# Loading and transposing the first attention group in other pieces, in a kernel of attention and four experts

## The chip, the cores and the metric

The kernel runs on one core of a Trainium2 chip. The metric is the device time of one execution, in microseconds. Beside the timed runs one execution was profiled; its trace gives each instruction's start and duration on the engines: PE (matrix multiplication), PEld (loading of PE's stationary operand), DVE (vector), ACT (activation functions), POOL (general purpose) and SP (here only issuing transfers). PSUM is the memory into which PE writes; SBUF is the working memory.

## The reference

Two steps. The first is attention for 4 batches and 8 heads over 768 positions with 64 elements per head. Heads 0, 2 and 6 ("retrieval") attend causally to everything; the others ("streaming") to the first 4 positions and a window of 64.

```python
scores = scale * np.matmul(q, k.transpose(0, 1, 3, 2))
stream_keep = causal & (is_sink | in_win)
a = np.exp(scores - max); a = a / (sum(a) + 1e-9)
attn_out = np.matmul(a, v)
```

The second feeds the 3072 resulting rows of 512 elements through 4 experts and adds them with normalised weights p:

```python
h = np.maximum(x @ w1[e], 0.0)          # 512 -> 1024
out += p[:, e:e + 1] * (h @ w2[e])      # 1024 -> 512
```

## The kernel before, in words

Attention is done in eight groups: a batch b and one half c of its 768 positions (384 queries). Group 0 is batch 0, first half. The experts ("MoE") work on the transposed attention output xT of a group, in four chunks of 128 features (ct 0 to 3); head h lands in chunk h % 4, half h // 4. PE runs one order, written out at build time: first group 0's attention alone, then the experts' matmuls with the later groups' attention steps put between them by a planner that adds up estimated durations. All engines run in the order in which the instructions are recorded; a semaphore holds an instruction, and all behind it on its engine, until its inputs and its buffer are ready.

**Loads.** Group 0's q and k are loaded as float32 through the queues of SP and ACT, one transfer per head, each a row of 64 elements (256 bytes) per partition and tile (`rows_of`, lines 411 and 424). The tiles q32 and k32 lie in hA, which later holds expert activations. Values and weights go through POOL's queue, which converts to float16 on the way: `load_v` (lines 304 and 310), `load_w1` (line 335, two halves per expert) and `load_w2` (lines 357 and 362). POOL issues them in the order of the text: v of head 0, then the masks bC and bS (lines 457 to 509), v of heads 2, 1, 3, 4, 6, 5, 7, then w1(0) and w2(0), some memsets, w1(1). `landed` makes POOL wait for a transfer before it asks for more. A queue has eight completion semaphores in turn, so a transfer is issued only when the one eight before it has landed.

**Group 0's attention.** `transposes(hp)` (lines 576 to 626) takes the pair of heads 2hp and 2hp+1: three transpositions of 128x128 float32 for q and three for k on PE, into a bank of PSUM, then copies to float16: q to qT, the keys of a retrieval head to kR, those of a streaming head to kS (with the first four positions repeated as "sinks", line 626). `scores(h)` (line 693) multiplies keys and queries, adds the mask as another matmul (line 705) and takes the exponential on ACT (line 711, es). `values` multiplies by v: for retrieval heads with a column of ones that gives the sum (line 756), then `rs`, its reciprocal and a product on DVE (lines 781 to 785), and `x_transposes` (line 805) turns the result back into xT. For streaming heads the product (line 828) comes with the sum in the other half of the partitions; ACT takes Ln and Exp(-) of it (lines 846 and 856) and DVE multiplies (line 851). Heads 3 and 4 share one Exp over 128 partitions (line 861). `sink_row` (line 318) copies four rows of v. `warm_up` (line 448) issues matmuls on zeros where PE would wait.

PSUM banks come from three pools: pA (4, scores and transposes), pV (2, values) and pO (2, warm-up, values of the second half, x_transposes and later expert output).

**Order in group 0 before:** transposes(0), scores(0), transposes(1), scores(2), scores(1) with values(0), transposes(2), scores(3) with values(2), x_transposes(0), scores(4), transposes(3), values(1), scores(5) with values(3), scores(6) with values(4), scores(7) with values(6), values(5), x_transposes(6) and values(7). Then expert 0's first layer starts (line 1095), its second layer is line 1116. Group 1's q and k are loaded as float16 in runs of three consecutive positions and transposed by matmuls with the identity (line 579).

Of the kernel before, what the change touches and what calls it, by code (L numbers as in the profile page):

```python
# [11 lines left out]
FP32 = mybir.dt.float32  # L12
# [7 lines left out]
def kernel(  # L20
# [33 lines left out]
    nc = tc.nc  # L54
# [260 lines left out]
    def sink_row(h):  # L315

        t = v_tiles(0, 0, h)
        nc.vector.tensor_copy(
            out=t[0:NS, :, own_v(h)],
            in_=v_s32[:, h : h + 1, :].to_broadcast([NS, TC, D]),  # L320
        )
# [10 lines left out]
    def load_w1(e, f0, f1):  # L332
        x = moe_w1[e].rearrange("(u c d) f -> u d c f", u=2, c=DMP)
        for u in range(2):
# [65 lines left out]
    def rows32(n):  # L400
        x = hA[:, n * 6 * H * D : (n + 1) * 6 * H * D].bitcast(FP32)
        return x.rearrange("p (j h d) -> p j h d", j=3, h=H)
# [3 lines left out]
    for h in range(H):  # L406
        if h == 2:
            nc.sync.dma_start(
                out=v_s32, in_=v[0, :, 0:NS, :].rearrange("h r d -> r h d")
            )  # L410
        nc.sync.dma_start(out=k32[:, :, h, :], in_=rows_of(k, 0, h, 0))
        if h == HP:

            nc.scalar.add_instruction(
                mybir.InstLoadActFuncSet(
                    name=nc.get_next_instruction_name(),
                    engine=ENG.Activation,
                    act_func_set_id=[x.name for x in SETS].index(
                        "natural_log_exp_and_others"
                    ),  # L420
                )
            )
        eng = nc.scalar if h < HP else nc.sync
        eng.dma_start(out=q32[:, :, h, :], in_=rows_of(q, 0, h, 0))
# [8 lines left out]
    nc.vector.memset(warm.bitcast(FP32), 0.0)  # L433
    nc.vector.memset(eps, 1e-9)
# [5 lines left out]
    zero(nc.vector, kS[:, 0, :, :, :])  # L440
# [14 lines left out]
    def mask_c(x, keep, drop):  # L455

        gp.memset(x, keep)
# [7 lines left out]
    def mask_s(x, n, keep, drop):  # L465

        gp.memset(x, keep)
        gp.affine_select(
            out=x, in_=x, compare_op=ALU.is_ge, fill=drop,
            base=R0, pattern=[[0, n], [1, TQ]], channel_multiplier=-1,  # L470
        )
        gp.affine_select(
            out=x, in_=x, compare_op=ALU.is_ge, fill=drop,
            base=NW - 1 - R0, pattern=[[0, n], [-1, TQ]], channel_multiplier=1,
        )
        gp.memset(x[0:R0, :, :], drop)
        gp.memset(x[0:NS, :, 0:TK], keep)
# [28 lines left out]

    mask_c(bC, 0.0, -60000.0)
    mask_s(bS[:, 0:2, :], 2, 0.0, -60000.0)
    gp.tensor_copy(out=bS[:, 2, :], in_=bS[:, 1, :])
    load_v(0, 0, [2, 1, 3, 4, 6, 5, 7])  # L510
    load_w1(0, 0, F)
# [46 lines left out]
    def attention(b, c):  # L558
# [8 lines left out]
        def transposed(x, hp):  # L567

            if first or hp > 1:
                ps = bank()  # L570
            else:
                ps = pV.tile([P, 512], FP32, name="pV", bufs=2)
            for j in range(3):
                o = ps[:, j * P : (j + 1) * P]
                if first:
                    nc.tensor.transpose(o, x[:, j, 2 * hp : 2 * hp + 2, :], ident32)
                    continue
                for u in range(2):
                    nc.tensor.matmul(
                        out=o[u * D : (u + 1) * D, :],  # L580
                        lhsT=x[:, 2 * hp + u, j, :],
                        rhs=ident16,
                        start=True,
                        stop=True,
                    )
            return ps

        def transposes(hp):
            both_at_once = [] if first else [transposed(x, hp) for x in (qt16, k16)]
            for x, is_k in ((q32 if first else qt16, 0), (k32 if first else k16, 1)):  # L590
                ps = transposed(x, hp) if first else both_at_once[is_k]
                if not is_k:
                    op = nc.scalar.copy if first and hp < 2 else nc.vector.tensor_copy
                    op(out=rows_in_order(qTs[b, c][:, hp, :]), in_=cols(ps))
                    if first:
                        yield t_ns
                    continue
                for u in range(2):
                    h = 2 * hp + u
                    r = slice(u * D, (u + 1) * D)  # L600
                    if RETR[h]:
                        nc.vector.tensor_copy(  # L602
                            out=rows_in_order(
                                kR[i][r, c, RH.index(h), :, :].rearrange(
                                    "r t x -> r (t x)"
                                )
                            ),
                            in_=cols(ps[r, :]),
                        )
# [3 lines left out]
                    if first:  # L613
                        x_in = x_in.rearrange("r (t x) -> r t x", x=TK)
                    else:
                        x_in = x_in.rearrange("r (j t p) -> r j t p", j=3, t=TC)
                        x_out = x_out.rearrange("r t (p j) -> r j t p", j=3)
# [8 lines left out]
                    op(out=sinks, in_=src.to_broadcast([D, TC, NS]))  # L626
                yield 2 * t_ns if first else 3 * t_ns

        def rows_in_order(x):

            return x if first else x.rearrange("r (p j) -> r j p", j=3)

        def cols(x):
            x = x[:, 0:CH]
            return x if first else x.rearrange("r (j p) -> r j p", j=3)

# [42 lines left out]

        es_of = {}  # L680
# [130 lines left out]
        def values(h):  # L811
# [30 lines left out]
            pair = first and h in (3, 4)  # L842
            if not pair or u == 0:
                rc_of[0] = att.tile([P, CH], FP32, name="rc", bufs=2)
            rc = rc_of[0]
# [12 lines left out]
            elif u == 0:  # L858
                scale_of[0] = scale
            else:  # L860
                nc.scalar.activation(out=rc, in_=rc, func=AF.Exp, scale=-1.0)
                later(scale_of[0], g)
# [805 lines left out]
```

## Time and profile before

| | |
|---|---|
| median of 3 runs | 376.27 us (376.0 to 377.43) |
| profiled execution | 377.82 us, span 376.1 us |
| PE busy | 367.1 us (98%) |
| DVE, ACT, POOL busy | 281.6, 227.3, 112.9 us |
| first expert matmul (line 1095) | 21.50 us |
| last wait of PE for weights | about 54.6 us |
| software queue (POOL), hardware queue of SP | 85824 and 36276 packets |

Times in the trace are in microseconds from the start of the span. In a timeline the columns are start, time from the first start to the last end of the merged instructions, engine, line, operation, output<-input, shapes and types, number, and in brackets the idle time of the engine before it and what ended it. In a view of waits a line is: who waited for whom, total, number of waits, longest. In a chain a piece is start, duration and what ran. A group's view of one line gives the shortest, median and longest duration in nanoseconds and the first and last start. PE's ends are modelled: matmuls overlap, so spacing between starts is the better price of one.

### The profile page before, as it was taken

How to read it: one execution, taken by the hardware profiler on the slowest of the kernel's cores; microseconds unless marked ns; L12 is line 12 of the kernel's file. 1: busy time of each engine (PE TensorE's matmuls, PEld its weight loads, DVE VectorE, ACT ScalarE, POOL GpSimd, SP SyncE). 2: the span in 40 equal slices, each digit the busy share in tenths (PEclk: the TensorE clock that was granted, in tenths of full speed). 3: DMA queues.
4: the chain of work that ended last, by engine and by line, in shares of the span. 5: the costliest groups of instructions: out<-in, count | busy, mean ns of one | idle time of the engine just before them, and what ended most of it. 6: DMA issues, size and time to landing. Idle time of an engine off the chain costs nothing.

```text
span 376.1 us, 10310 instructions
## 1 busy us (share of the span) xinstructions
PE 367.1 (98%) x4221; PEld 312.4 (83%) x4221; DVE 281.6 (75%) x589; ACT 227.3 (60%) x475; POOL 112.9 (30%) x155
## 2 busy tenths in 40 slices
PE   8889999999999999999999999999999999999996
PEld 4755556568998999999989899988899998998996
DVE  7774768697788569868657858957767968989882
ACT  3863478557785785765676955774678362450630
POOL 8923664793058038115601650320000000000000
DMA  8999999999599579988904991971220200300101
GB/s 157 159 208 207 179 186 194 180 201 121 90 104 164 97 83 133 153 111 63 205 12 61 169 156 16 131 129 12 68 72 2 92 24 2 114 2 0 58 3 58
DMA packets 123748, 39.25 MB, mean 104 GB/s; under 512 B 113728, under 2 KB 116356, under 8 KB 123700
## 3 DMA queue, kind: packets, MB, share of 16 engines
q0 software_dynamic: 85824, 19.01, 58.6%
q1 hardware_dynamic: 36276, 19.18, 23.3%
q8 instruction: 33, 0.54, 0.7%
q10 hardware_dynamic: 1600, 0.39, 0.5%
q14 instruction: 15, 0.12, 0.1%
HBM read 44.89 MB, written 6.34 MB: 136 GB/s over the span
## 4 chain that ended last, share of the span: by engine, by line
PE 78%; DMA 12%; DVE 5%; POOL 3%; issue 1%; ACT 0%; DVEq 0%; POOLq 0%
PE pO L1409 29%; PE pA L1229 20%; PE pO L1258 9%; PE pO L1116 5%; DMA q<-in_q_dram 5%; PE pA L693 4%; DMA w2sb<-in_moe_w_dram 4%; PE pA L1095 3%; DMA w1sb<-in_moe_w_dram 2%; PE pV L1258 2%; PE pA L1258 2%; DVE xs L1180 2%; PE pV L828 2%; PE pV L756 2%; DMA xT<-x_pair 1%
## 5 line engine op out<-in xcount | busy, mean ns | idle before, releaser
L1409 PEld LDWEIGHTS <-hA 128*128 128x128 f16 x1104 | 104.9, 98 | 11.9
L1229 PE MATMUL pA<-xs,w1sb 128*128 128x256 f16 x768 | 97.1, 272 | 0.0
L1229 PEld LDWEIGHTS <-w1sb 128*128 128x128 f16 x768 | 71.7, 98 | 7.3
L1409 PE MATMUL pO<-w2sb,hA 128*128 128x256 f16 x640 | 76.8, 272 | 0.0
L711 ACT ACTIVATE es<-pA 128x384 f16<-128x384 f32 (+2 forms) x122 | 59.2, 512 | 26.4 <-PE pA L693 23.2
L1238 ACT ACTIVATE hA<-pA 128x512 f16<-128x512 f32 x96 | 57.2, 597 | 29.6 <-PE pA L1229 27.3
L306 POOL DMA_DIRECT2D vS<-in_v_dram x30 | 29.6, 986 | 113.7 <-PE pV L828 110.5
L1409 PE MATMUL pO<-tsb,hA 128*128 128x256 f16 x464 | 56.8, 272 | 0.0
L1180 DVE TENSOR_TENSOR xs<-xT,pB 128x1024 f16<-128x1024 f16 (+1 forms) x49 | 47.0, 977 | 3.7 <-DMA xT<-x_pair 3.7
L1014 DVE TENSOR_TENSOR hA<-hA 128x1024 f16<-128x1024 f16 x60 | 39.4, 684 | 0.6 <-PE pO L1409 0.3
L1108 ACT ACTIVATE hA<-pA 128x384 f16<-128x384 f32 (+1 forms) x64 | 22.2, 385 | 20.3 <-PE pA L1095 20.2
L1258 PEld LDWEIGHTS <-w1sb 128*128 128x128 f16 x512 | 31.3, 98 | 2.1 <-DVE xs L1014 0.8
L1095 PE MATMUL pA<-xT,w1sb 128*128 128x384 f16 (+1 forms) x256 | 30.4, 272 | 2.0 <-DMA w1sb<-in_moe_w_dram 1.9
L1116 PE MATMUL pO<-w2sb,hA 128*128 128x512 f16 x128 | 30.6, 379 | 0.1
L1095 PEld LDWEIGHTS <-w1sb 128*128 128x128 f16 x256 | 19.5, 98 | 11.0 <-issue 2.6
L1429 ACT COPY s<-pO 128x256 f32<-128x256 f32 x31 | 11.5, 372 | 27.3 <-PE pO L1409 21.8
L851 DVE TENSOR_TENSOR xT<-pV,rc 64x384 f16<-64x384 f32 x37 | 20.5, 554 | 9.3 <-ACT rc L856 6.8
L722 DVE TENSOR_TENSOR es<-es,mS 128x384 f16<-128x384 f16 (+1 forms) x40 | 13.8, 344 | 18.0 <-ACT es L711 17.9
L846 ACT ACTIVATE rc<-pV,eps 64x384 f32<-64x384 f32 x37 | 21.3, 575 | 7.0 <-PE pV L828 6.4
L1275 DVE CUSTOM_DVE_ANT_0 hA<-pO,s 128x512 f16<-128x512 f32 x26 | 17.7, 688 | 9.9 <-PE pO L1258 8.5
L1268 ACT COPY s<-pO 128x512 f32<-128x512 f32 x39 | 22.7, 588 | 3.2 <-PE pO L1258 3.0
L693 PE MATMUL pA<-qT,kR 128*128 128x128 f16 (+2 forms) x141 | 23.1, 261 | 0.4 <-DVE kR L602 0.4
(170 smaller groups left out, 527.6 us busy)
## 6 DMA issues: line engine op xcount, KB each, us to landing
pB<-p_rows SPq DMA_DIRECT2D x10, 512.0 KB
out_dram<-o SPq DMA_DIRECT2D x19, 256.0 KB
w1sb<-in_moe_w_dram POOLq DMA_DIRECT2D x8, 512.0 KB, 9.2
w2sb<-in_moe_w_dram POOLq DMA_DIRECT2D x4, 1024.0 KB, 13.3
vS<-in_v_dram POOLq DMA_DIRECT2D x30, 112.0 KB, 4.8
k_rows<-in_k_dram POOLq DMA_DIRECT2D x18, 128.0 KB, 5.1
q<-in_q_dram POOLq DMA_DIRECT2D x18, 128.0 KB, 6.4
vR<-in_v_dram POOLq DMA_DIRECT2D x24, 48.0 KB, 5.5
```

Of the source, the lines that this page charges most:

```text
L306: gp.dma_start(out=t[:, :, own_v(h)], in_=windows_of(v, b, h, c))
L693: nc.tensor.matmul(out=ps[:, o : o + nq], lhsT=key_tile(b, c, h, t), rhs=qTs[b, c][:, hp, q0 : q0 + nq], start=(n == 0 or not first), stop ...
L711: nc.scalar.activation(out=es[:, 0:cols], in_=ps[:, 0:cols], func=AF.Exp, scale=SC)
L1014: nc.vector.tensor_tensor(out=out, in0=a, in1=b, op=ALU.subtract)
L1095: nc.tensor.matmul(out=pss[ft][:, 0:cols_n], lhsT=w1_tile(e, ct, ft), rhs=x[:, ct, :], start=(n == 0), stop=(n == DMP - 1),)
L1116: nc.tensor.matmul(out=ps_o, lhsT=hs[:, ft, j * P : (j + 1) * P], rhs=w2sb[:, e * FTP + ft, :], start=(ft == 0), stop=(ft == FTP - 1),)
L1180: nc.vector.tensor_tensor(out=o, in0=xin, in1=pb.to_broadcast([P, DMP, n, P]), op=ALU.mult)
L1229: nc.tensor.matmul(out=ps[:, f * PC : (f + 1) * PC], lhsT=w1_tile(e, ct, f0 + f), rhs=xs[:, ct, :], start=(ct == 0), stop=(ct == DMP - 1),)
L1238: nc.scalar.activation(out=blocks[:, b0 : b0 + 2, k0 : k0 + 2, :].rearrange("p t f x -> p f t x"), in_=ps.rearrange("p (f t x) -> p f t x" ...
L1258: nc.tensor.matmul(out=ps[:, f * P : (f + 1) * P], lhsT=w_tile(e, w[:, ct, :], f), rhs=a[:, ct, :], start=(first and f == 0 and ct == 0), ...
L1268: nc.scalar.copy(out=kept[n], in_=ps)
L1409: nc.tensor.matmul(out=ps, lhsT=a[:, k, :], rhs=b(k), start=(first and k == 0), stop=(k == KT - 1), skip_group_check=not first,)
```

## The change

All of it lies in what runs up to the end of group 0's attention, apart from the form of group 1's transpositions.

- q and k of heads 2 to 7 are loaded a pair of heads at a time, three consecutive positions in a run of 768 bytes (`pair_of_triples`). Heads 0 and 1 keep their form. There are 10 q and k transfers instead of 16.
- The transposes of those pairs become six float32 matmuls of 64x128 with the identity per tensor, written with a step of three words so that PSUM holds positions in order. They use pO's two banks instead of pA's. Group 1's write the same way, and the copies out of PSUM become contiguous.
- transposes(1) stands before scores(0), transposes(2) before scores(1), transposes(3) before scores(3). The copies of the sinks of heads 1 and 3 are put off behind scores(0).
- sink_row does two heads in one copy where they follow each other.
- w1(0) is asked for in halves: one after v(3), one after v(6). The masks get their zeros from a DVE memset, are built at half the width and copied; one copy goes to DVE. The zeroing of kS is cut into four.
- Heads 1 and 4, and heads 3 and 5, share an Exp; head 7 has its own. values(4) and values(3) change places, and x_transposes(6) comes ahead of values(7).

```diff
-    def sink_row(h):
-        t = v_tiles(0, 0, h)
+    def sink_row(h, n=1):
+        s0, step = SH.index(h), SH[min(SH.index(h) + 1, NSH - 1)] - h or 1
+        x = v_s32[:, h : h + step * (n - 1) + 1 : step, :]
+        x = x.rearrange("r (t s) d -> r t s d", t=1)
         nc.vector.tensor_copy(
-            out=t[0:NS, :, own_v(h)],
-            in_=v_s32[:, h : h + 1, :].to_broadcast([NS, TC, D]),
+            out=vS[0:NS, 0, :, s0 : s0 + n, own_v(h)],
+            in_=x.to_broadcast([NS, TC, n, D]),
         )
...
+    def pair_of_triples(eng, x, dst, h):
+        if h == 0:
+            for u in range(2):
+                eng.dma_start(out=dst[0][:, :, u, :], in_=rows_of(x, 0, u, 0))
+            return
+        eng.dma_start(
+            out=dst[1][:, h - 2 : h, :, :].rearrange("p h j d -> p h (j d)"),
+            in_=x[0, h : h + 2, 0:CH, :].rearrange("h (p j) d -> p h (j d)", j=3),
+        )
...
-    for h in range(H):
+    for h in range(0, H, 2):
...
-        nc.sync.dma_start(out=k32[:, :, h, :], in_=rows_of(k, 0, h, 0))
+        pair_of_triples(nc.sync, k, k32, h)
...
-        eng.dma_start(out=q32[:, :, h, :], in_=rows_of(q, 0, h, 0))
+        pair_of_triples(eng, q, q32, h)
...
+    nc.vector.memset(early[:, 1536:2272].bitcast(FP32), 0.0)
...
-    zero(nc.vector, kS[:, 0, :, :, :])
+    for t in range(TC):
+        zero(nc.vector, kS[:, 0, t : t + 1, :, :])
...
-    mask_c(bC, 0.0, -60000.0)
-    mask_s(bS[:, 0:2, :], 2, 0.0, -60000.0)
-    gp.tensor_copy(out=bS[:, 2, :], in_=bS[:, 1, :])
-    load_v(0, 0, [2, 1, 3, 4, 6, 5, 7])
-    load_w1(0, 0, F)
+    mask_c(bC, -60000.0)
+    mask_s(bS, 0.0, -60000.0)
+    nc.vector.tensor_copy(out=bS[:, 2, :], in_=bS[:, 1, :])
+    load_v(0, 0, [2, 1, 3])
+    load_w1(0, 0, F, 0)
+    load_v(0, 0, [4, 6])
+    load_w1(0, 0, F, 1)
+    load_v(0, 0, [5, 7])
     load_w2(0)
...
-            if first or hp > 1:
+            if first and hp:
+                ps = pO.tile([P, 512], FP32, name="pO", bufs=2)
+            elif first or hp > 1:
                 ps = bank()
...
+            natural = ps[:, 0:CH].rearrange("r (x j) -> r j x", j=3)
             for j in range(3):
-                o = ps[:, j * P : (j + 1) * P]
-                if first:
-                    nc.tensor.transpose(o, x[:, j, 2 * hp : 2 * hp + 2, :], ident32)
+                o = natural[:, j, :]
+                if first and hp == 0:
+                    nc.tensor.transpose(
+                        ps[:, j * P : (j + 1) * P], x[0][:, j, :, :], ident32
+                    )
                     continue
                 for u in range(2):
                     nc.tensor.matmul(
                         out=o[u * D : (u + 1) * D, :],
-                        lhsT=x[:, 2 * hp + u, j, :],
-                        rhs=ident16,
+                        lhsT=x[1][:, 2 * hp - 2 + u, j, :] if first else x[:, 2 * hp + u, j, :],
+                        rhs=ident32 if first else ident16,
...
-                    op(out=sinks, in_=src.to_broadcast([D, TC, NS]))
+                    src = src.to_broadcast([D, TC, NS])
+                    if first and hp < 2:
+                        put_off.append(lambda o=sinks, i=src: nc.scalar.copy(out=o, in_=i))
+                    else:
+                        op(out=sinks, in_=src)
...
-            pair = first and h in (3, 4)
+            pair = first and {1: 1, 4: 1, 3: 3, 5: 3}.get(h)
...
             yield from transposes(0)
+            yield from transposes(1)
             yield from scores(0)
-            sink_row(1)
-            sink_row(3)
-            yield from transposes(1)
+            for x in put_off:
+                x()
+            sink_row(1, 2)
             yield from scores(2)
-            sink_row(4)
-            sink_row(5)
+            yield from transposes(2)
+            sink_row(4, 2)
             sink_row(7)
             yield from both(scores(1), values(0))
-            yield from transposes(2)
+            yield from transposes(3)
             yield from both(scores(3), values(2))
             x_transposes(0)
             yield from scores(4)
-            yield from transposes(3)
             yield from values(1)
-            yield from both(scores(5), values(3))
-            yield from both(scores(6), values(4))
+            yield from both(scores(5), values(4))
+            yield from both(scores(6), values(3))
             yield from both(scores(7), values(6))
             yield from values(5)
-            at_once = behind.pop()
-            v_steps = values(7)
-            yield next(v_steps)
             x_transposes(6)
-            at_once[1]()
-            yield from v_steps
+            yield from values(7)
```

More of the change, by code (lines that the diff above doesn't have):

```diff
@@ L330, in sink_rows, with load_w1 @@
             )
-    def load_w1(e, f0, f1):
+    def load_w1(e, f0, f1, *us):
         x = moe_w1[e].rearrange("(u c d) f -> u d c f", u=2, c=DMP)
-        for u in range(2):
+        for u in us or range(2):
             gp.dma_start(
@@ L401, in rows32 @@
         x = hA[:, n * 6 * H * D : (n + 1) * 6 * H * D].bitcast(FP32)
-        return x.rearrange("p (j h d) -> p j h d", j=3, h=H)
+        x, y = x[:, 0 : 6 * D], x[:, 6 * D :]
+        x = x.rearrange("p (j h d) -> p j h d", j=3, h=2)
+        return x, y.rearrange("p (h j d) -> p h j d", j=3, h=H - 2)
+    def pair_of_triples(eng, x, dst, h):
[7 more added lines that the diff above has]
+        )
     q32, k32 = rows32(0), rows32(1)
     v_s32 = early[0:NS, 0:1024].bitcast(FP32).rearrange("p (h d) -> p h d", h=H)
-    for h in range(H):
+    for h in range(0, H, 2):
         if h == 2:
@@ L451, in warm_up, with mask_c @@
             )
-    def mask_c(x, keep, drop):
-        gp.memset(x, keep)
+    def mask_c(x, drop):
         for i in range(2):
@@ L463, in mask_c, with mask_s @@
             )
-    def mask_s(x, n, keep, drop):
-        gp.memset(x, keep)
+    def mask_s(x, keep, drop):
+        y = x[:, 1, :]
         gp.affine_select(
-            out=x, in_=x, compare_op=ALU.is_ge, fill=drop,
-            base=R0, pattern=[[0, n], [1, TQ]], channel_multiplier=-1,
+            out=y, in_=y, compare_op=ALU.is_ge, fill=drop,
+            base=R0, pattern=[[1, TQ]], channel_multiplier=-1,
         )
         gp.affine_select(
-            out=x, in_=x, compare_op=ALU.is_ge, fill=drop,
-            base=NW - 1 - R0, pattern=[[0, n], [-1, TQ]], channel_multiplier=1,
-        )
-        gp.memset(x[0:R0, :, :], drop)
-        gp.memset(x[0:NS, :, 0:TK], keep)
+            out=y, in_=y, compare_op=ALU.is_ge, fill=drop,
+            base=NW - 1 - R0, pattern=[[-1, TQ]], channel_multiplier=1,
+        )
+        gp.memset(y[0:R0, :], drop)
+        gp.memset(y[0:NS, 0:TK], keep)
+        gp.tensor_copy(out=x[:, 0, :], in_=y)
         gp.affine_select(
@@ L593, in transposes @@
                     op = nc.scalar.copy if first and hp < 2 else nc.vector.tensor_copy
-                    op(out=rows_in_order(qTs[b, c][:, hp, :]), in_=cols(ps))
+                    op(out=qTs[b, c][:, hp, :], in_=ps[:, 0:CH])
                     if first:
@@ L602, in transposes @@
                         nc.vector.tensor_copy(
[L603 to L606, printed above, removed]
+                            out=kR[i][r, c, RH.index(h), :, :].rearrange(
+                                "r t x -> r (t x)"
                             ),
-                            in_=cols(ps[r, :]),
+                            in_=ps[r, 0:CH],
                         )
@@ L612, in transposes @@
                     x_in, x_out = ps[r, 0:CH], kS[r, c, :, n, R0:P]
[L613 to L617, printed above, removed]
+                    x_in = x_in.rearrange("r (t x) -> r t x", x=TK)
                     nc.vector.tensor_copy(out=x_out, in_=x_in)
@@ L625, in transposes @@
                     src = src.rearrange("r (o x) -> r o x", o=1)
-                    op(out=sinks, in_=src.to_broadcast([D, TC, NS]))
-                yield 2 * t_ns if first else 3 * t_ns
[L629 to L635, printed above, removed]
+                    src = src.to_broadcast([D, TC, NS])
[3 more added lines that the diff above has]
+                        op(out=sinks, in_=src)
+                yield 2 * t_ns if first else 3 * t_ns
         def score_tiles(h):
@@ L678, in score_tiles @@
             ]
+        put_off = []
         es_of = {}
@@ L841, in values @@
             r, o = half(u), half(1 - u)
-            pair = first and h in (3, 4)
+            pair = first and {1: 1, 4: 1, 3: 3, 5: 3}.get(h)
             if not pair or u == 0:
-                rc_of[0] = att.tile([P, CH], FP32, name="rc", bufs=2)
-            rc = rc_of[0]
+                rc_of[pair] = att.tile([P, CH], FP32, name="rc", bufs=2)
+            rc = rc_of[pair]
             nc.scalar.activation(
@@ L858, in values @@
             elif u == 0:
-                scale_of[0] = scale
+                scale_of[pair] = scale
             else:
                 nc.scalar.activation(out=rc, in_=rc, func=AF.Exp, scale=-1.0)
-                later(scale_of[0], g)
+                later(scale_of[pair], g)
                 later(scale, g)
```

## The prediction

> **What bounds the kernel now.** The profiled execution took 377.82 us for a span of 376.1 us; the three timed runs have their median at 376.27 us, so the sum below is a shift, worked out in the profile's own times and put on the median. I read the page's chain first, then its first 60 us in order of time, since the change touches nothing later.
>
> ```profile
> PE 78%; DMA 12%; DVE 5%; POOL 3%; issue 1%; ACT 0%; DVEq 0%; POOLq 0%
> ```
> ```profile
> 12.53 8.84 DMA w1sb<-in_moe_w_dram
> ...
> 22.40 11.30 DMA q<-in_q_dram
> ...
> 35.01 5.72 DMA q<-in_q_dram
> 41.02 13.57 DMA w2sb<-in_moe_w_dram
> 54.59 0.04 issue
> 54.63 1.02 PE pO L1116 x4
> ```
>
> From 12.5 to 54.6 us the chain goes through transfers, afterwards through PE with hardly a gap. But the chain alone overstates DMA: what matters is how long PE really stood still for it. The wait view of PE, 4 to 22 us and then 22 to 57 us:
>
> ```profile
> PE pA L1095 <- DMA w1sb<-in_moe_w_dram: 1.1, 1, 1.1
> PE pV L756 <- ACT es L711: 1.0, 1, 1.0
> ```
> ```profile
> PE pA L1095 <- DMA w1sb<-in_moe_w_dram: 0.8, 1, 0.8
> PE pV L756 <- ACT es L711: 0.2, 1, 0.2
> PE pV L579 <- DMA q<-in_q_dram: 0.2, 1, 0.2
> ```
>
> After the first MoE matmul (21.50 us) PE lost 0.80 + 0.16 us to transfers, and some 0.25 us more just before 54.63. So the end can come at most 1.2 us earlier by earlier transfers alone; beyond that it follows the start of the MoE. That start, 21.50 us, was gated twice almost at once: w1(0) landed at 21.37, and the last input of its third matmul (xT chunk 1, head 5's scaling) ended at 21.58, which would have allowed 21.26. So the case is decided by when group 0's attention now ends. The timelines of DVE and ACT show what set that:
>
> ```profile
> 9.49 0.83 DVE L318 CAST vS<-early 4x256 f16<-4x256 f32 x3
> 10.35 0.16 DVE L781 TENSOR_SCALAR rs<-pV 128x3 f32<-128x3 f32 x1
> ...
> 11.03 0.55 DVE L594 CAST qT<-pA 128x384 f16<-128x384 f32 x1
> 11.49 0.54 DVE L618 CAST kS<-pA 64x384 f16<-64x384 f32 x1
> ...
> 12.72 0.71 ACT L711 ACTIVATE es<-pA 128x320 f16<-128x320 f32 x2 [0.35 <-PE pA L705]
> 13.78 0.58 ACT L846 ACTIVATE rc<-pV,eps 64x384 f32<-64x384 f32 x1 [0.35 <-PE pV L828]
> ...
> 21.29 0.52 ACT L856 ACTIVATE rc<-rc 64x384 f32<-64x384 f32 x1
> ```
>
> DVE has no idle gap from 8.9 to 16.2 us; head 4's scores wait for its copies, and from head 4's first exponential (12.72) ACT runs nearly without a break to head 7's Exp (21.81).
>
> **The change, part by part.**
>
> *Transfers.* The small hardware-queue packets take 18.4 ns of an engine each (5400 of them are 47.9% of 16 engines in the first 13 us). 4608 packets of 256 bytes become 1536 of 768. From below such a packet costs the same 18.4 ns; from above its share by bytes of the output stores' (88.5 us for 830 packets of 2.31 KB, 107 ns), 35 ns. Saved: (84.8 - 28.3 to 54.5) / 16 = 1.9 to 3.5 us of all engines. The software queue runs full from 12.5 us, so the later loads land about that much earlier. This is worth the 1.2 us of PE waits and no more: what is late next is PE itself.
>
> *POOL.* Two memsets (0.33, 0.36) leave, the two 320-column selects (0.46, 1.46) become 160 columns wide, the 0.35 and 0.25 memsets shrink, and the copy of 0.31 stays under another name. The value loads begin at 4.6 to 5.8 us, not 6.98; w1(0)'s first half is requested after three of them (2.15), at 6.8 to 8, not 11.92, the second two loads later. w1(0) should then land at about 16. Worth 0.24 us (21.50 to 21.26) if nothing else moves. The loads of v(4) and v(6) stand behind half of w1(0) on that queue, v(5) and v(7) behind all of it; their readers come after 14 and 19 us, so 0. SP issues 7 q and k loads of 0.49 instead of 12, ACT 3 instead of 4: no price, since PE is busy with fillers until 4.73 either way.
>
> *PE.* Per pair, six f32 transpositions of 128x128 become twelve f32 matmuls of 64x128. The trace has no plain f32 matmul. The two nearest rows: f16 64x128, six in 0.36 (L579: 0.219 each, so 0.028 apart), and f32 transpositions, six in 0.85 (0.273 each, 0.115 apart).
>
> ```profile
> L579 PE MATMUL pV<-ident,q x12: 219/219/243, 33.8 to 37.7; 128*64 128x128 f16 x12
> ...
> L576 PE MATMUL pA<-early,hA x24: 272/273/446, 4.7 to 13.2; 128*128 128x128 f32 x24
> ```
>
> From below 0.028 each; from above twice the transposition, 0.24. I take 0.115, the row of the same type: six in 0.69, against 0.69 for a whole pair's six before.
>
> *The trace has only the rows above; a page speaks against this step.* The Trainium skill's "TensorE: Matmul & The Clock Gate", Terms, says transpose mode is 4x faster for FP32, and "TensorEngine Tiling (Array Packing)", Restrictions, that column tiling switches that mode off. Four times the f16 row is 0.112, my value; four times the transposition row is 0.46, which would make a pair 5.5 us and the whole some 10 us slower. No row decides between them.
>
> *The walk through group 0.* Heads 0 and 1's transpositions are unchanged (4.73 to 6.24; the next can issue at 5.97). Pair 1's twelve now come before scores(0): 5.97 + 2 x 0.69 + 0.2 (PE is still slow there: the first six took 1.51, later sixes 0.85) = 7.55. Five fillers (0.28) and scores(0) (0.67, before at 6.88) end at 8.5; eight fillers (0.45) and scores(2) (0.73) at 9.7. That is no later than before (8.92 + 0.73), since head 2's keys are copied earlier. Then pair 2's q: 9.7 + 0.69 + 0.22 = 10.6.
>
> *DVE, where the order bites.* From 10.6 DVE does in order: q 0.46, keys 0.47, sinks 0.19, keys 0.48, sinks 0.20, the sink rows of v 0.57 and 0.29, head 0's three steps 0.68, pair 3's q 0.55 (all start to start in the rows above): 3.9 us. Only then has x_transposes(0) both its input and its bank, because the transposes took over pO's two buffers: 14.5, before 11.87. It stands ahead of scores(4) on PE, so head 4's first exponential starts 0.85 later (11.87 to 12.72), at 15.35, which is 2.6 us later than before. Sharing Exp by four heads instead of two saves one activation, 0.55 with its gap; the rest of ACT's stretch (9.09 us) stays: Exp of head 7 ends at 15.35 + 8.54 = 23.9. Heads 3 and 5 are scaled after their common Exp (1.15 earlier) in 2 x 0.57: 23.9; the first MoE matmul may lead that by 0.32: 23.6, 2.1 us later than 21.50.
>
> *Edits I cost at nothing.* Group 1's twelve copies on DVE fall from 0.80 to about 0.55 (contiguous now); no PE wait on DVE stands between 22 and 57 us, so nothing is gained; its 48 f16 matmuls now write every third word of PSUM, which no row prices: 0 is the nearest row's (the same matmul), 48 x 0.028 = 1.3 us if it doubles, which I keep in the range. The new DVE memset of 368 words (by 0.27 for 256: 0.39), the split of kS (0.15), the copy of a mask block (0.2): DVE was idle 0.77 before 6.28, so covered, just. If that cover fails, all of the walk slips by as much.
>
> **Sum.** Start +2.1, less the 1.2 us of transfer waits that the later start and the earlier landings cover: +0.9 us. 376.27 + 0.9 = 377.2 us (378.7 for a profiled execution). With 0.028 per matmul pair 2's q is done at 9.3 (scores(2) gated by DVE as before), the start is 22.25 (+0.75): -0.45. With 0.24 it is done 2.25 later than taken: +3.1.
>
> **The rivals.**
> - *Cheap f32 matmuls* (0.028): 375.8 us. For it: at f16 two 64-wide ones overlap (0.028 apart, 128x128 fillers 0.056). Against: f32 weights take 143 ns to load for 128 columns, f16 ones 98.
> - *Slower by the f32 matmuls* (0.24 and up, no overlap of the halves): 379.4 us or more. It decides from 0.16 each on, where the end passes 1.9 us. For it: f32 has no fast row here at all.
> - *Faster by an earlier attention*: the pulled-in w1(0) and the shared Exp let the MoE start by 20.8, at most 374.3 us. It needs x_transposes(0) no later than before, 11.9, so DVE would have to do those 3.9 us before it; against it is the copy order above.
> - *Transfers do not come earlier*: then 54.63 stays as a floor, and only the cheap case changes, to 376.3.
>
> **How the numbers follow.** Forecast (0.06 to 0.16 each) 0.46, cheap 0.23, dear 0.23, early start 0.08. A measurement here tells apart from no change about 0.5%, 1.9 us. Slower: four fifths of the dear case and a tenth of the forecast, 0.24; faster: the early start, 0.08; the rest 0.68. The range leaves out the early start and the dear case's upper half: 375.0 to 379.4 us.
>
> **What would show it.** Right: PE's new group at the transposing line with starts 0.11 apart; a PE wait on DVE at x_transposes(0), near 14.5; head 4's exponential past 14; no PE wait on w1(0), and none above 0.3 us on a DMA after it; first MoE matmul at 23 to 24. Wrong: the MoE starting before 21.5 (the walk on DVE is too long), or starts above 0.2 apart (dear), or waits on transfers left after 25 us.

## The result: 6.0 us slower, and where the time lies in the profile after

The changed kernel takes 382.12 us (median of 4 runs, 381.22 to 383.24), the kernel before beside it 376.13 us. The ratio is 1.0153, 95% interval 1.0118 to 1.0188. The prediction, 377.2 us in a range of 375.0 to 379.4, was wrong. The profiled execution took 382.11 us, its span 380.4.

From the page after, the clock that PE was granted and the chain by engine:

```profile
PEclk9899999999999999999999999999999999999999
...
PE 93%; DVE 3%; ACT 1%; DMA 1%; issue 0%; ACTq 0%
```

DMA's share of the chain is 1% instead of 12%: the loss isn't in waiting for transfers. The second slice of the clock row has an 8, so the clock fell somewhere in it (mean 0.996 over the span); the kernel before had a mean clock of 1.000. The waits of PE from 4 to 28 us, and what DVE and POOL did at that time (timelines of 9 to 17 us):

```profile
PE pO L820 <- DVE qT L619: 2.0, 1, 2.0
PE pA L1106 <- DVE xT L866: 1.1, 1, 1.1
PE pV L771 <- ACT es L726: 0.3, 1, 0.3
```
```profile
10.80 0.56 DVE L619 CAST qT<-pO 128x384 f16<-128x384 f32 x1 [0.95 <-PE pO L604]
...
12.58 0.17 DVE L649 CAST kS<-pO 64x16 f16<-64x16 f32 x1
12.78 2.42 DVE L320 CAST vS<-early 4x512 f16<-4x512 f32 x2
15.23 0.16 DVE L796 TENSOR_SCALAR rs<-pV 128x3 f32<-128x3 f32 x1
...
15.91 0.55 DVE L619 CAST qT<-pO 128x384 f16<-128x384 f32 x1
```
```profile
11.67 0.60 POOL L381 MEMSET kR<- 128x576 f32 x1
12.19 1.19 POOL L381 MEMSET kS<- 128x1280 f32 x1
13.29 0.14 POOL L381 MEMSET vR<- 128x9 f32 x1
13.34 2.23 POOL L381 MEMSET vS<- 32x1280 f32 x3
```

The 2.0 us at L820 is x_transposes(0) waiting for pair 3's q copy to free a bank, the wait that the prediction named. What was not foreseen is the length of DVE's walk: two sink-row copies (L320) took 2.42 us. (The 1.1 us at L1106 is the third expert matmul waiting for head 5's scaling, with which the prediction's walk through group 0 ends.) The group's view of the line gives shortest, median and longest in ns:

```profile
L320 DVE CAST vS<-early x3: 466/496/2022, 9.4 to 14.7; 4x512 f16<-4x512 f32 x2, 4x256 f16<-4x256 f32 x1
```

The same shape took 0.50 us at 9.35 and 2.02 at 12.78, while POOL ran its memsets for group 1 back to back. In the kernel before, sink rows and memsets didn't meet: the copies started between 7.4 and 10.0, and POOL's timeline has

```profile
13.88 0.63 POOL L379 MEMSET kR<- 128x576 f32 x1
14.39 1.22 POOL L379 MEMSET kS<- 128x1280 f32 x1
```

What the gap then did to PE, in the timeline after, and in a table of 2 us stretches (busy time of PE, PEld, DVE, ACT and POOL with counts, granted clock, DMA share, GB/s):

```profile
16.51 0.33 PE L820 MATMUL pO<-ident,x_one 128*64 128x128 f16 x3 [2.00 <-DVE qT L619]
...
16.95 0.47 PE L720 MATMUL pA<-early,ident 128*128 128x320 f16 x1
...
17.64 0.69 PE L843 MATMUL pV<-es,vS 128*128 128x160 f16 x4
...
26.50 5.29 PE L1106 MATMUL pA<-xT,w1sb 128*128 128x384 f16 x30 [1.11 <-DVE xT L866]
31.62 5.34 PE L1127 MATMUL pO<-w2sb,hA 128*128 128x512 f16 x24
```
```profile
14.00:16.00 2.00, 0.51 (x10) 0.29 (x8) 1.90 (x6) 0.79 (x2) 1.94 (x4) 1.00 1.39 186
16.00:18.00 2.00, 1.49 (x12) 1.33 (x13) 1.90 (x6) 0.47 (x2) 0.73 (x2) 0.72 1.40 158
18.00:20.00 2.00, 2.00 (x16) 1.70 (x15) 0.81 (x2) 1.34 (x3) 1.68 (x3) 0.50 1.12 212
20.00:22.00 2.00, 1.97 (x20) 1.56 (x19) 0.79 (x2) 1.92 (x5) 0.00 (x0) 0.93 1.13 212
```

After the idle 2.0 us the granted clock was 0.72, then 0.50, and head 4's mask matmul took 0.47 instead of 0.30 us. Not every execution has this fall: of the four timed ones two have a mean clock of 0.996 (382.11 and 382.13 us) and two of 1.000 (381.22 and 383.24). The last new price is at the transposing line, float32 in group 0 and float16 in group 1:

```profile
L604 PE MATMUL pO<-early,hA x72: 272/273/324, 6.6 to 13.5; 128*64 128x128 f32 x72
...
L604 PE MATMUL pV<-ident,q x12: 297/314/314, 38.2 to 42.5; 128*64 128x128 f16 x12
```

The trace shows 72 starts for 36 float32 matmuls. The float16 ones take 314 ns where the contiguous ones took 219.

One figure makes all runs below comparable: when expert 0's second layer starts (first matmul of `pO<-w2sb`), and how much of the profiled execution's time comes after it. Before: 26.95 us, and 377.82 - 26.95 = 350.87. After: 31.62 and 350.49. So in the two profiles the start moves by +4.67 and the rest by -0.38, together 4.29. The medians differ by 6.0, since the profiled execution of before was 1.7 us above its median.

### The profile page after: what moved, and what is told of

It reads as the page before. It is cut to its first block, busy times and chain, and to the rows that moved or that the text cites. A ratio compares the mean times of both kernels' runs of the same rounds, so it can differ in the third digit from the quotient of the medians.

```text
span 380.4 us, 10407 instructions
## 1 busy us (share of the span) xinstructions
PE 371.6 (98%) x4275; PEld 316.2 (83%) x4275; DVE 280.4 (74%) x592; ACT 227.1 (60%) x474; POOL 110.5 (29%) x153
## 4 chain that ended last, share of the span: by engine, by line
PE 93%; DVE 3%; ACT 1%; DMA 1%; issue 0%; ACTq 0%
PE pO L1420 31%; PE pA L1240 22%; PE pO L1269 9%; PE pA L1106 7%; PE pO L1127 7%; PE pA L708 5%; PE pV L1269 2%; PE pV L771 2%; PE pV L843 2%; PE pA L1269 2%; DMA hA<-in_q_dram 1%; PE pO L604 1%; DVE vS L320 1%; DVE xs L1191 1%; PE pA L1512 0%; ACT es L726 0%
## 5 line engine op out<-in xcount | busy, mean ns | idle before, releaser
L1106 PE MATMUL pA<-xT,w1sb 128*128 128x384 f16 (+1 forms) x256 | 30.7, 273 | 1.2 <-DVE xT L866 1.1
L1106 PEld LDWEIGHTS <-w1sb 128*128 128x128 f16 x256 | 19.5, 98 | 10.4 <-issue 2.3
L1440 ACT COPY s<-pO 128x256 f32<-128x256 f32 x31 | 11.5, 373 | 27.5 <-PE pO L1420 23.1
```

The costliest lines, as they stand in the source:

```text
L1106: nc.tensor.matmul(out=pss[ft][:, 0:cols_n], lhsT=w1_tile(e, ct, ft), rhs=x[:, ct, :], start=(n == 0), stop=(n == DMP - 1),)
```

## The experiments

Four explanations were put against each other: (A) the new order of group 0, in which transposes(2) and (3) stand ahead of x_transposes(0); (C) the collision of the sink-row copies with POOL's memsets; (D) group 1's strided writes to PSUM; (E) the clock that falls after the PE gap. Names that begin with a are edits of the changed kernel (also c_all and d_first), the others of the kernel before. The kernel before ran beside each set of runs, with medians from 376.01 to 376.55, so differences of medians between two sets are uncertain by some tenths. The starts of the second layer and the times:

| run | start of second layer, us | rest, us | median (runs) | ratio to before, 95% interval |
|---|---|---|---|---|
| before, profile of the prediction | 26.95 | 350.87 | 376.13 (4) | |
| after | 31.62 | 350.49 | 382.12 (4) | 1.0153 [1.0118, 1.0188] |
| a_order | 29.17 | 350.52 | 379.70 (6) | 1.0120 [1.0087, 1.0152] |
| a_memset | 28.83 | 350.53 | 379.57 (4) | 1.0091 [1.0078, 1.0104] |
| a_group1 | 30.74 | 349.71 | 380.99 (4) | 1.0132 [1.0118, 1.0147] |
| a_fill | 30.98 | 350.48 | 381.28 (4) | 1.0139 [1.0126, 1.0152] |
| a_two | 29.11 | 349.74 | 378.79 (5) | 1.0057 [1.0045, 1.0069] |
| c_all | 28.43 | 349.51 | 378.26 (5) | 1.0047 [1.0031, 1.0062] |
| d_first | 28.20 | 349.54 | 377.78 (7) | 1.0024 [0.9987, 1.0061] |
| b_again | 26.05 | 350.35 | 376.4 (1) | |
| b_group1 | 26.87 | 350.01 | 377.29 (12) | 1.0020 [0.9999, 1.0041] |
| b_pool | 33.91 | 349.55 | 383.20 (6) | 1.0164 [1.0126, 1.0202] |
| c_pool | 32.04 | 349.51 | 382.83 (4) | 1.0161 [1.0134, 1.0187] |
| c_pool_exp | 33.05 | 349.54 | 382.75 (4) | 1.0145 [1.0106, 1.0184] |
| d_late | 27.68 | 349.53 | 376.81 (10) | 1.0005 [0.9986, 1.0023] |
| d_late_exp | 26.65 | 350.08 | 376.68 (10) | 1.0009 [0.9996, 1.0021] |

**The order undone (a_order).** In the changed kernel:

```diff
             yield from scores(2)
-            yield from transposes(2)
             sink_row(4, 2)
             sink_row(7)
             yield from both(scores(1), values(0))
-            yield from transposes(3)
+            yield from transposes(2)
             yield from both(scores(3), values(2))
             x_transposes(0)
             yield from scores(4)
+            yield from transposes(3)
             yield from values(1)
```

> The changed kernel with one thing undone: the transposes of pair 2 stand again behind scores(1) and values(0), those of pair 3 behind scores(4), and the sink rows of heads 4, 5 and 7 ahead of both, as before. All float32 matmuls, pO's banks, loads and Exp pairs stay. Theory A (DVE's order holds PE at x_transposes(0)): x_transposes(0) falls from 16.5 to about 12.5 us, PE's 2.0 us wait on DVE goes, head 4's first exponential starts near 13.6 instead of 17.5, the sink rows run before POOL's memsets and take 0.5, and the time falls by 3 to 4.5 us, to about 378.4. Theory B (the dearer float32 matmuls make group 0 longer, whatever the order): head 4's exponential stays past 16 and the time falls by at most 1 us.

2.4 us less, short of theory A's 3 to 4.5. The sink rows now run at 9.6 us, no copy longer than 0.56, although the memsets still run from 12.0; x_transposes(0) comes at 13.29. But part of the gain is given back at once, in ACT's timeline:

```profile
14.13 0.71 ACT L726 ACTIVATE es<-pA 128x320 f16<-128x320 f32 x2 [0.35 <-PE pA L720]
16.51 0.58 ACT L861 ACTIVATE rc<-pV,eps 64x384 f32<-64x384 f32 x1 [1.68 <-PE pV L843]
```

values(1) waits behind pair 3's matmuls. This run mixes A and C, since it also parts copies and memsets.

**The memsets moved (a_memset).** POOL's three kinds of memsets for group 1 go behind the loads of group 1's q and k, to 19.8 us; DVE's order isn't touched.

```diff
     load_w2(0)
-    zero(gp, kR[0][:, 1, :, :, :])
-    zero(gp, kS[:, 1, :, :, :])
-    one_values(gp, 1)
...
     load_triples(q, qt16, 0, 1, 0, HP)
+    zero(gp, kR[0][:, 1, :, :, :])
+    zero(gp, kS[:, 1, :, :, :])
+    one_values(gp, 1)
```

> The changed kernel with POOL's memsets for group 1 (kR, kS, the ones of vR and vS, 3.9 us from 11.7 us on) put behind the requests for group 1's first k and q. Theory C (the sink-row copy of heads 4 and 5 took 2.02 us instead of 0.50 because POOL's memsets ran beside it): the copy takes 0.5, x_transposes(0) starts at about 15.0 instead of 16.5, PE's wait on DVE shrinks from 2.0 to 0.5, and the time falls by 1.5 to 2.5 us, to about 380. If the copy waits for something else (a transfer, its own pattern), it stays near 2.0 and the time near 382.1.

The group's view of the copies, and DVE's timeline:

```profile
L320 DVE CAST vS<-early x3: 276/414/588, 9.3 to 13.0; 4x512 f16<-4x512 f32 x2, 4x256 f16<-4x256 f32 x1
```
```profile
12.69 0.62 DVE L320 CAST vS<-early 4x512 f16<-4x512 f32 x2
```

The two copies take 0.62 instead of 2.42 us, at the same time of the span. Head 4's exponential starts at 15.43 instead of 17.52, PE's wait at x_transposes(0) falls from 2.00 to 0.20, the clock stays at 1.00, and the median falls by 2.55 us. C is confirmed, and with it goes E, which hangs on the gap.

**Group 1 contiguous (a_group1).** Group 1's matmuls write each third to its own 128 columns as before, and its copies take the strides again (group 0 unchanged).

```diff
-                o = natural[:, j, :]
+                o = natural[:, j, :] if first else ps[:, j * P : (j + 1) * P]
```

> The changed kernel with group 1's transposes written to PSUM without a step and copied with one, as in the kernel before. Theory D (PE writes every third word of PSUM at about half the rate): six of group 1's matmuls take 0.34 instead of 0.53, a pair's twelve 0.46 instead of 0.78, and the time falls by 1.2 us, to 380.9. If the step costs nothing on the path, the time stays at 382.1 or rises a little by the slower copies on DVE.

```profile
L604 PE MATMUL pV<-ident,q x12: 219/219/243, 37.3 to 41.3; 128*64 128x128 f16 x12
```

219 ns again; 1.13 us less in the median, and 0.78 in the rest after the second layer's start (350.49 to 349.71). D is confirmed. The earlier start of the second layer, 30.74, isn't D's: in this execution the clock stayed at 1.00 although the gap was nearly the same. PE's timeline:

```profile
16.53 0.33 PE L834 MATMUL pO<-ident,x_one 128*64 128x128 f16 x3 [1.81 <-DVE qT L619]
```

**Fillers in the gap (a_fill).** 18 matmuls on zeros ahead of x_transposes(0) keep PE busy while DVE is late.

```diff
             yield from both(scores(3), values(2))
+            warm_up(bank(), 18, 256)
             x_transposes(0)
```

> The changed kernel with 18 fillers of 256 columns (0.107 each, 1.9 us) put on PE ahead of x_transposes(0), where PE stood still for 2.0 us. x_transposes(0) stays at 16.5, since it waits for DVE. Theory E (the gap also cost time afterwards, through the granted clock of 0.50 to 0.72 from 16 to 20 us): the clock stays at 1.00, scores(4) to values(4) run at 0.30 and 0.41 instead of 0.47 and 0.69, ACT's wait of 0.61 for head 4's values goes, and the time falls by 0.6 to 1.2 us. If ACT's own work sets that stretch, the time stays at 382.1.

```profile
16.00:18.00 2.00, 1.87 (x22) 1.52 (x21) 1.96 (x6) 0.43 (x2) 0.99 (x2) 1.00 1.34 170
18.00:20.00 2.00, 2.00 (x27) 1.80 (x25) 1.01 (x4) 1.89 (x6) 1.61 (x3) 1.00 1.12 211
```

The clock stays at 1.00. x_transposes(0) comes even later (16.76), yet the second layer starts 0.64 us earlier and the median is 0.84 lower. E is worth about that where the clock falls: in a_group1, where it didn't fall, x_transposes(0) came at 16.53, as in the profile after (16.51), and the second layer started 0.88 us earlier.

**Both mended (a_two).** The edits of a_memset and a_group1 together.

> The changed kernel with both POOL's memsets moved back and group 1's transposes written without a step. If the two costs add (2.5 and 1.1 us measured one at a time), 382.1 - 3.6 = 378.5 us, and what is left over the kernel before, 2.5 us, belongs to the order of group 0 with its float32 matmuls. If they hide one another, it stays above 379.

378.79 us, 3.3 less than after; the two effects add up to within 0.35 (2.55 + 1.13 = 3.68). What is left over before (376.55 beside it) is 2.2 us.

**The order of what is left (c_all, d_first).** c_all is a_two with

```diff
             yield from scores(2)
-            yield from transposes(2)
             sink_row(4, 2)
             sink_row(7)
             yield from both(scores(1), values(0))
-            yield from transposes(3)
+            yield from transposes(2)
...
             yield from values(1)
+            yield from transposes(3)
```

and d_first is c_all with, further,

```diff
             yield from transposes(0)
-            yield from transposes(1)
             yield from scores(0)
+            yield from transposes(1)
```

> The changed kernel with the memsets moved, group 1's transposes written contiguously and, against the earlier kernel that had both (378.8 us), the order of group 0 undone where it crosses DVE: transposes(2) behind scores(1) and values(0), transposes(3) behind values(1), sink rows ahead. Order theory (the rest over before is the copies of pair 2 standing ahead of the step that transposes head 0's result): head 4's first exponential comes at 13 to 14.2, the experts start at 21.5 to 23, 376.0 to 377.5 us. Rival (the rest is the price of the f32 matmuls, of the 768-byte transfers that gate pair 1, and of later heads' keys): 378.3 or more, with the lost time in a PE or ACT wait for pair 3.

> The kernel of 378.26 us (changed kernel with memsets moved, group 1 contiguous, transposes(2) and (3) put back), with scores(0) ahead of transposes(1) again as in the kernel before. First-scores theory (transposes(1) ahead of scores(0), with its wait for pair 1's transfer, costs what is left): head 0's first exponential at 7.2 to 7.8 instead of 8.86, head 4's at 12.4 to 13.2, 376.4 to 377.4 us. Rival (the twelve f32 matmuls per pair instead of six transpositions cost it, wherever they stand): head 2's scores wait for pair 1 instead, head 4's first exponential stays at 13.4 or later and the time at 377.9 to 378.5.

378.26 and 377.78 us: 0.5 us each in the medians, 0.68 and 0.23 in the starts; the intervals in the table overlap from step to step. So the order (A) is worth 0.5 us or so once C is mended. In c_all the steps on DVE came as the order theory had them, but the time did not; it lies at the rival's edge. Head 4's exponential starts 1.88 us earlier than in a_two (13.84 against 15.72), head 7's Exp only 0.69 (22.72 against 23.41). In d_first head 0's exponential comes at 7.02 and head 4's only at 13.61, which is what the rival said; the time lies between the two forecasts. ACT's timeline of d_first shows the place:

```profile
13.61 0.71 ACT L740 ACTIVATE es<-pA 128x320 f16<-128x320 f32 x2 [0.34 <-PE pA L734]
...
16.09 0.44 ACT L740 ACTIVATE es<-pA 128x320 f16<-128x320 f32 x1 [1.16 <-PE pA L734]
```

Wherever pair 3's twelve float32 matmuls stand, head 5's scores wait behind them: in each of these orders ACT lost over a microsecond there, at values(1) in a_order (1.68) and at head 5's exponential in c_all and d_first (1.15, 1.16). So the last 1.4 us (377.78 against 376.34 for before beside it; the interval reaches from -0.5 to +2.3, so they are not clear of nothing) are put down in the main to the twice as many matmuls. That is argued from these waits, not shown; no run had six matmuls in this order. Another part can be read from the traces: behind the new zeros, the zeroing of kS in pieces and the mask copy, DVE's first key copy starts at 5.94 instead of 5.43 (b_again), and scores(0) at 6.48 instead of 6.04, so some 0.4 us are lost before any of these matmuls.

**Before again (b_again).** The same kernel, without an edit, profiled once more.

> The kernel before, unchanged, for a second trace. The first profiled execution took 377.82 us where the other runs took about 376.0. Theory: the 1.7 us are in its first 55 us, where PE waited for transfers (1.1 us on w1(0), 0.80 on w1(2), 0.16 on q): in an execution of 376.0 us these waits are shorter and the MoE starts before 21.5 us. Rival: the difference lies behind 55 us or at the ends of the span.

PE's timeline of this execution:

```profile
20.42 5.79 PE L1095 MATMUL pA<-xT,w1sb 128*128 128x384 f16 x32 [0.74 <-DMA w1sb<-in_moe_w_dram]
26.05 5.34 PE L1116 MATMUL pO<-w2sb,hA 128*128 128x512 f16 x24
```

The experts start 1.08 us earlier than in the profile of the prediction, and the execution lies at the median. So the profile from which the prediction was read had a late group 0. Of the 1.42 us between the two executions 0.90 lie before the second layer's start. The lateness begins with the first six transpositions, 0.85 us from 4.54 in b_again, but in the profile of the prediction

```profile
4.73 1.51 PE L576 MATMUL pA<-early,hA 128*128 128x128 f32 x6
```

although the granted clock reads 1.00 there in both; and w1(0)'s transfer took 8.84 us there, 7.63 in b_again.

**Strided writes alone (b_group1).** The kernel before, with its copies for group 1 made contiguous and

```diff
                 o = ps[:, j * P : (j + 1) * P]
+                if not first:
+                    o = ps[:, 0:CH].rearrange("r (x j) -> r j x", j=3)[:, j, :]
```

> The kernel before with group 1's transposes written to PSUM with a step of three words and copied without one, alone. Theory D: a pair's twelve matmuls take 0.78 instead of 0.46, 1.2 us in all, of which the waits for transfers after them hide up to 1.0: 0.2 to 1.2 us slower, 376.2 to 377.2. Rival: the contiguous copies on DVE (0.55 instead of 0.80) are worth as much: no change, 376.0.

0.7 us more in the median, the interval from 0 to 1.5. Each matmul took 314 ns here too. Its profile has no PE wait for a transfer left after 22 us, where b_again has three; so part of the price seems to hide behind those waits, which no run shows by itself.

**The POOL part alone (b_pool, c_pool, d_late).** Three steps on the kernel before. b_pool takes the masks at half width, the zeros from DVE, and w1(0) in halves between the value loads:

```diff
+    nc.vector.memset(early[:, 1536:2272].bitcast(FP32), 0.0)
...
-    load_v(0, 0, [2, 1, 3, 4, 6, 5, 7])
-    load_w1(0, 0, F)
+    load_v(0, 0, [2, 1, 3])
+    load_w1(0, 0, F, 0)
+    load_v(0, 0, [4, 6])
+    load_w1(0, 0, F, 1)
+    load_v(0, 0, [5, 7])
```

c_pool moves the memsets besides, as in a_memset. d_late is c_pool with the two load lines of before restored, so that only the early request is undone.

> The kernel before with POOL's part of the change alone: masks at half width with zeros from DVE, kS zeroed in four, w1(0) requested in halves between the value loads. Theory: w1(0) lands near 17, the MoE starts when its inputs are ready (21.3), and the later waits for transfers (0.80, 0.16 and 0.25 us in the profile of before) go: 0.5 to 1.4 us faster, 374.6 to 375.5. Rival: the copies of v(5), v(7) or the transfers of q and k come later for it and group 0 ends later: 376.5 or more.

> The kernel before with the POOL part of the change (half-width masks, zeros from DVE, w1(0) in halves between the value loads), and POOL's three kinds of group 1 memsets moved behind the loads of group 1's q and k, so that they no longer run beside DVE's copies of the sink rows. Collision theory (the memsets beside the sink-row copies are all that cost the POOL part alone its 6.5 us): no sink-row copy over 0.7 us, the experts start at 20.4 to 21.3, 375.0 to 376.5 us. Rival (something else of the POOL part costs: the new work on DVE before 6 us, or w1(0)'s packets delaying q, k or v): a PE wait of over 1 us on a DMA or DVE stays before 20 us and the time stays above 378.

> The kernel before with the POOL part of the change but for the early request: w1(0) is asked for whole behind all value loads again (about 9.6 us, before 11.9), and the memsets stay moved. Competition theory (w1(0)'s packets, asked for from 6.9 us, hold up the 256-byte packets of q and k of pair 3): no PE wait over 0.6 us on q and k before 20 us, the hardware queue's packets done by 13 us, experts start at 20 to 21.5, 375.0 to 376.8 us. Rival (another piece of the POOL part holds up q and k): PE still waits 2 us or more for pair 3, 379 or more.

b_pool missed by 7.7 us. DVE's timeline and PE's waits:

```profile
9.76 4.94 DVE L318 CAST vS<-early 4x256 f16<-4x256 f32 x3
```
```profile
PE pO L810 <- DVE x_one L790: 3.3, 1, 3.3
```

One of the copies took 4.07 us (group's view), from 10.63 to 14.70. POOL's memsets ran from 11.70 to 15.3, so they held it for most of that time but not at its start, when POOL was issuing transfers. c_pool took that away (longest copy 0.42, the last begun at 9.6) and is as slow as before it, 382.83. Now PE waits elsewhere; waits, and PE's timeline:

```profile
PE pA L581 <- DMA hA<-in_q_dram: 4.2, 1, 4.2
```
```profile
16.68 1.51 PE L581 MATMUL pA<-early,hA 128*128 128x128 f32 x6 [4.25 <-DMA hA<-in_q_dram]
```

Pair 3's q lands at 16.6. The hardware queue's packets per 2 us from 6 us on show why. Before: 1448, 1065, 1092, 8 and none after 14 us. c_pool: 1079, 907, 126, 720, 375, 272, so that it isn't done by 16. From 10 to 12 us, where only 126 got through, the software queue moved 0.36 MB in 175 packets; in the kernel before it moved 0.14 MB in 1166 then, beside 1092 of the hardware queue. d_late has no such wait (1308 packets from 10 to 12, 30 from 12 to 14) and 376.81 us. So with 256-byte pieces the early request of w1(0) is a loss of 6 us, the clock's fall behind the gap included. In the changed kernel the same request does no such harm: its larger pieces are through by 10 us (940 and 610 packets from 6 to 10, none from 10 on). That the two edits need each other is read from these packets; no run has the larger pieces without the early request.

**The shared Exp (c_pool_exp, d_late_exp).** The change's pairing of the Exp, with the order of values that it needs, on c_pool and d_late.

```diff
-            pair = first and h in (3, 4)
+            pair = first and {1: 1, 4: 1, 3: 3, 5: 3}.get(h)
...
-            yield from both(scores(5), values(3))
-            yield from both(scores(6), values(4))
+            yield from both(scores(5), values(4))
+            yield from both(scores(6), values(3))
```

> The previous kernel with the change's pairing of the Exp (heads 1 and 4, heads 3 and 5, with values(4) ahead of values(3) and the transposing step of head 6 ahead of values(7)). If ACT's stretch from head 4's first exponential to head 7's Exp sets the start of the experts, one activation less gives 0.3 to 0.6 us: 374.5 to 376.1. Rival: the start is set by w1(0) or by PE and DVE steps, then no difference to the previous kernel beyond 0.3, or a loss of up to 0.6 because heads 1 and 3 are scaled later, behind the Exp that they share.

> The previous kernel with the change's pairing of the Exp. If ACT's stretch sets the start of the experts: 0.3 to 0.6 us less than the previous kernel, 374.5 to 376.3. Rival: w1(0) or DVE sets it, no difference beyond 0.3.

382.75 against 382.83, 376.68 against 376.81: no difference that these runs can tell. In d_late_exp the second layer starts 1.03 us earlier than in d_late, but the rest is 0.55 longer, and group 0's length varies between executions by nearly as much (26.05 and 26.95 for the same kernel); d_late's first six transpositions took 1.51 us, d_late_exp's 0.85. No kernel here beats the one before.

## Why the prediction was wrong

In the terms of the sum, from before at its median (b_again, start 26.05, rest 350.35) to after (31.62, 350.49): +5.57 and +0.14, 5.7 of the 6.0 us.

- **Price of the float32 matmuls: right.** Twelve in 1.53 us, 0.11 from one to the next, nearly as taken ("I take 0.115"). Neither the cheap nor the dear rival happened, nor the 0.46 that the prediction worked out from a page.
- **The walk over PE and DVE: right, where nothing disturbs it.** Pair 2's q began to be copied at 10.80 (10.6 foreseen). With the memsets out of the way (a_memset) x_transposes(0) came at 14.62 (14.5) and head 4's exponential at 15.43 (15.35). The start of the second layer, 28.83, is 1.88 us past 26.95, foreseen +2.1. Pair 1 waited for its transfer until 6.60 instead of 5.97, which PE made good in its fillers but for 0.2.
- **Transfer waits after the experts' start: right.** No wait of PE on a transfer is left there. The sum allowed 1.2 us for it. b_again has three such waits (0.63, 0.32, 0.28), and the kernels with neither waits nor strided writes have a rest of 349.5 instead of its 350.35: it was worth 0.83.
- **The step that failed: "sink rows of v 0.57 and 0.29", with POOL's part "worth 0.24 ... if nothing else moves".** I let the value loads come up to 2.4 us forward on POOL and followed only the transfers on that queue. The memsets behind them came forward too, from 13.88 to 11.67, and the sink rows, which my own walk had put behind 12.4, ran into them. That they would meet could be worked out from before (13.88 less 2.4 is 11.5); what a meeting costs stood in no line that the prediction shows. The term measured 2.42 instead of 0.86, and with what follows from it 2.55 us of the 6.0.
- **Following from it: the clock.** The prediction named a PE wait at x_transposes(0) without a length and priced the matmuls after it at full speed. On the undisturbed walk that wait is 0.20 us (a_memset) and the clock stays. Behind the 2.00 us of the profile they ran at 0.50 to 0.72: 0.64 to 0.84 us (a_fill), part of the 2.55.
- **Mis-sized: the strided writes of group 1, taken at 0.** The bound that I kept for the range, 1.3 us, was nearly right: 1.13 by a_group1's median, 0.78 in its rest. I had taken the row of the same matmul, written contiguously; the group's view of after says 314 ns instead of 219. The Trainium skill's "PSUM — Partial Sum Buffer", Specifications, says that any pattern that isn't contiguous slows matmuls markedly, and the float16 rows here agree. The float32 ones, with the same step, took 273 ns, no more than a contiguous float32 transposition; no run has them contiguous.
- **Mis-sized: the base.** I put the shift, worked out against a profile 1.55 us above the median that I had, on the median. That execution started its experts 1.08 us later than b_again, and both of them wait for w1(0) there, which the changed kernel doesn't. Nor does a quick start help the changed kernel: where transposes(1) stands first, pair 1 waits for its transfer until 6.51 to 6.86 in every trace, however fast the first six transpositions ran (PE stood still 0.96 us for it in a_two), a wait that the sum didn't have. Against a usual execution the undisturbed shift of the start is 28.83 - 26.05 = 2.78, not 2.1.
- **The sum again.** Foreseen +0.9; the collision with its clock 2.55, the strided writes 1.13, the base 0.68 (2.78 less 2.1), the transfer waits 0.37 less than allowed: 5.6 of the measured 6.0. The 0.4 that is left is within what single executions of one kernel differ by.
- **The rivals.** The dear rival's time, 379.4, is nearer than mine, but its mechanism isn't what happened. I had no rival in which an engine off the path collides with one on it.

## What to carry to other kernels

When a load on a queue is pulled forward, everything behind it on that engine comes forward too: write down where each of its instructions, memsets included, will then run, and what the other engines do at that time. A wait of some 2 us on PE can cost more than its length, by a slower clock behind it (here 0.6 to 0.9 us, in some executions and not in others). And check a profile's own time against the median before putting a shift on it: what the profiled execution had late, the changed kernel may not share.

## What the runs showed that was not expected

- DVE copies of a few rows from float32 to float16 within SBUF, 0.27 to 0.5 us by themselves, took 2.02 us (after; 1.84 and 2.12 in a_group1 and a_fill) and 4.07 us (b_pool, the first 1.07 of them before the memsets) while POOL ran memsets without a gap; with the memsets elsewhere they took at most 0.59 and 0.42. In all four traces the copy ended 0.1 to 0.3 us after the end of the first memset of vS. DVE's copies out of PSUM beside the same memsets (12.10 us in after) kept their 0.56. The Trainium skill's "SBUF — State Buffer", Who interferes with whom, has copies and casts of DVE contend with POOL, when they run in a mode that uses both pairs of DVE's ports, for a pair that is held for a whole instruction, the loser waiting. This agrees in kind, though no run shows the mode of these copies; but the copies were held longer than the longest memset (1.19 us), as if DVE lost several turns in a row. Why, and what held the one in b_pool before the memsets, no run here settles.
- A PE gap of 2.0 us was enough for a granted clock of 0.50 over the next 2 to 4 us (after), and one of 1.81 us in a_group1 left it at 1.00; in c_pool, with 4.25 us, the clock was 0.70 within the gap and 0.50 behind it.
- Matmuls of 64x128 float16 went from 219 to 314 ns with a step of three words in PSUM; float32 ones with that step took 273, as long as contiguous float32 transpositions of 128x128.
- 256-byte packets of the hardware queue nearly stopped (126 in 2 us instead of 1092) when the software queue carried large ones.
